# Two groups' gate logits in one set of 512-column products, and two more alignment directives

## The chip, the cores and the metric

The kernel runs on one core of one Trainium2 chip. The metric is the device time of one execution in microseconds; of several runs the median is given. The engines are named as the profile names them: PE (TensorE; PEld its weight loads), DVE (VectorE), ACT (ScalarE), POOL (GpSimd), SP (SyncE, which issues most transfers).

## The reference

```python
# attention: 8 batches x 8 heads, 576 rows in chunks of 64, head size 64
scores = scale * np.matmul(q_c, k_c.transpose(0, 1, 2, 4, 3))
scores = scores - np.max(scores, axis=-1, keepdims=True)
attn = np.exp(scores)
attn = attn / (np.sum(attn, axis=-1, keepdims=True) + 1e-09)
out = np.matmul(attn, v_c)
...
# mixture of experts on its output: x is 4608 x 512, 8 experts, 512 -> 1024 -> 512
logits = x @ w_gate
expert_idx = np.argmax(logits, axis=1)
logits_shift = logits - logits.max(-1, keepdims=True)
probs = np.exp(logits_shift)
probs /= probs.sum(-1, keepdims=True) + 1e-09
gate_w = probs[np.arange(N), expert_idx]
for e in range(E):
    mask = expert_idx == e
    xe = x[mask]
    h = np.maximum(xe @ w1[e], 0.0)
    ye = h @ w2[e]
    out[mask] = gate_w[mask, None] * ye
```

Each row of x goes to the one expert with the largest logit.

## The kernel before, in words

The 4608 rows of x are 36 tiles of 128, taken as 18 groups of G = 2 tiles. The first part is a software pipeline over the groups (the loop at L1033, iteration g = 0 to 17), the second the experts' products, 256 rows and up to 128 more at a time. The order of all engines' work is written out by hand: each engine runs its instructions in the order in which the program issues them.

In iteration g, PE does in this order: scores(g) (L238, 32 products of 64 by 64, into psS); sel_ of group g - 3 (L991: the logits of two tiles, transposed, into psL); attn_t of group g - 1 (L274: eight transposes of the exponentials into psU and psV); x_t of group g - 2 (L310: eight transposes of the rows of x into psT and psQ); in some iterations routing's small products (L379 to L384); attn_v of group g - 1 (L286: attention times v, into psU, psV and, for the last of four head pairs, psT); and logits of group g - 2 (L322). A fp32 product stands in the trace as two matmuls, a transpose as one.

The gate's logits: x_t copies the transposed rows to SBUF (ACT, L312). logits_p multiplies each of the four 128-row pieces of a row's 512 features with its part of the gate's weights, in four column tiles of the array side by side, so that the four partial results lie in four groups of 32 partitions of psL, in columns 128 to 383. ACT copies them to lp (L1007); one iteration later sel_ turns them back into rows, into columns 0 to 127 and 384 to 511 of psL, and sums (DVE, L998) adds the four partial results. Groups make batches of 6, 6, 6, 6, 4, 4, 2 and 2 tiles; when sums has a batch's last group, its routing (route, L327) starts as a generator. Its steps are issued one by one between other work: `small_op` and `advance` take the next step of the first generator that stands at that kind of step, "v" for DVE, "a" for ACT, "t" for PE. A batch's steps fill two iterations. Then its tiles wait for store (L426), in which POOL scatters the rows of x with their gate weight and row number to xd in DRAM, two tiles at the top of each iteration, four in the last, the rest behind the loop. Ahead of that, where tiles wait, POOL copies one column of lp to a scrap tile (relay, L1037), which holds it until lp has been written.

x_out (L298 twice, then L301) divides attn_v's result by the sums that ACT copied (su, L264 and L265) and DVE inverted (ri, L266), and writes the group's rows of x. x_t of the next iteration reads these rows.

When the third batch is routed and its tiles have been stored, the generator early issues the gather of unit 0's rows (L547) into xg; behind the loop make_xt (L570) transposes them and unit 0's products (filler, L622 and L720 to L722) fill the gaps between the last groups' steps. SP issues the loads of q, k and v for coming groups, and in iterations 2 to 10 quarters of an expert's weights.

nc.tensor.addr_align(64, offset=48, max_nops=0) ahead of the scores of g = 3 (and one at L142) sets at which place, counted in instructions modulo 64, the next instruction of PE's code lies; the loader puts padding in between, and with max_nops=0 PE jumps over it with one branch. The second part begins at L1264 with the load of the number of units into registers.

Of the kernel before, what the change touches and what calls it, by code (L numbers as in the profile page):

```python
# [8 lines left out]
F32 = mybir.dt.float32  # L9
# [4 lines left out]
ALU = mybir.AluOpType  # L14
AX = mybir.AxisListType
# [3 lines left out]
P = 128  # L19
# [3 lines left out]
E = 8  # L23
NTILE = NT // P
G = 2
NG = NTILE // G
RB = 4
XB = 5
BATCHES = [6, 6, 6, 6, 4, 4, 2, 2]
NBAT = len(BATCHES)  # L30
NMAX = max(BATCHES)
# [15 lines left out]
def attn_moe_kernel(ctx: ExitStack, tc: tile.TileContext, q, k, v, wg, w, out):  # L47
    nc = tc.nc
# [69 lines left out]
    sp = c1.enter_context(tc.tile_pool(name="sp", bufs=2))  # L118
    sm = c1.enter_context(tc.tile_pool(name="sm", bufs=2))
# [31 lines left out]
    wg_sb = kv.tile([P, 4, 32], F32, name="wg_sb")  # L151
# [3 lines left out]
    first = [sum(BATCHES[:i]) for i in range(NBAT + 1)]  # L155
# [13 lines left out]
    ident = const.tile([P, P], F32, name="ident")  # L169
# [61 lines left out]
    def scores(g):  # L231
        ps = pair
        if g == 3:
            nc.tensor.addr_align(64, offset=48, max_nops=0)
        for i in range(G):
            for hp in range(4):
                for po, m, fo, pi, fi, at_ in quads(i, hp):
                    nc.tensor.matmul(ps[po, m, fo], qt[g][pi, i, fi], kb[g % NK][pi, i, fi],  # L238
                                     start=True, stop=True, tile_position=at_)
        return ps  # L240
# [19 lines left out]
    def soft_d():  # L260
        su = sm.tile([P, NH, 1], F32, name="su", bufs=2)
        ri = sm.tile([P, NH, 1], F32, name="ri", bufs=2)
        for i in range(G):
            nc.scalar.activation(su[:, 6 * i:6 * i + 6, 0], one["UV"[i]][:, i * 64:i * 64 + 326:65], AF.Copy, bias=1e-9)  # L264
            nc.scalar.activation(su[:, 12 + 2 * i:14 + 2 * i, 0], px3[:, i * 195:i * 195 + 66:65], AF.Copy, bias=1e-9)  # L265
        nc.vector.reciprocal(ri.rearrange("p h o -> p (h o)"), su.rearrange("p h o -> p (h o)"))  # L266
        return ri

    def attn_t(ex, banks="UV"):
        at = sp.tile([P, G, 4, 128], F32, name="at", bufs=1)  # L270
# [20 lines left out]
    def x_out(g, ri, xt):  # L291
# [5 lines left out]
        for i in range(G):  # L297
# [4 lines left out]
            o[:, :, 6:8, :], px3[:, 1:261].rearrange("p (i h d) -> p i h d", i=G, d=65)[:, :, :, 0:64],  # L302
            ri[:, 12:NH, :].rearrange("p (i h) o -> p i h o", i=G).broadcast_to([P, G, 2, 64]), ALU.mult)

    def x_t(g, xt):
        xT = sp.tile([P, 4, G * P], F32, name="xT1", bufs=1)
        for i in range(G):
            pxt = bank("TQ", [P, 4, 128])
            for kc in range(4):
                nc.tensor.transpose(pxt[:, kc, :], xt[:, (g * G + i) % RB, kc * 128:(kc + 1) * 128],  # L310
                                    ident)
            nc.scalar.copy(xT[:, :, i * P:(i + 1) * P], pxt)  # L312
        return xT

    pL = bank("L", [P, 512])
    pR = bank("K", [P, 512])

    def logits_p(g, xT):

        pp = pL[:, 128:128 + G * P]  # L320
        for kc in range(4):
            nc.tensor.matmul(pp[kc * 32:(kc + 1) * 32, :], wg_sb[:, kc, :], xT[:, kc, :],  # L322
                             start=True, stop=True, tile_position=(0, kc * 32))
        lp = sp.tile([P, G * P], F32, name="lp", bufs=2)
        return lp, pp

    def route(b, lg):  # L327
# [89 lines left out]
    relay = const.tile([P, 1], F32, name="relay")  # L417
# [14 lines left out]
    active = []  # L432
# [550 lines left out]
    st_e, st_l, st_x = {}, {}, {}  # L983
    casts = []
    lgs = [None]
    p4 = pL.rearrange("p (a t) -> p a t", t=P)

    def sel_(g):
        lp = st_l.pop(g)
        for i in range(G):  # L990
            nc.tensor.transpose(p4[:, 3 * i, :], lp[:, i * P:(i + 1) * P], ident)  # L991

    def sums(g):
        b = [i for i in range(NBAT) if first[i] <= g * G][-1]
        if g * G == first[b]:
            lgs[0] = sm.tile([P, NMAX, E], F32, name="lg", bufs=2)[:, 0:BATCHES[b], :]
        o = g * G - first[b]
        nc.vector.tensor_reduce(lgs[0][:, o:o + G, :],  # L998
                                p4.rearrange("p a (c e) -> p a e c", e=32)[:, 0::3, 0:E, :], AX.X, ALU.add)
        if (g + 1) * G == first[b + 1]:  # L1000
            r = route(b, lgs[0])
            active.append([r, next(r), False])

    def logits(g):
        if g in st_x:
            lp, pp = logits_p(g, st_x.pop(g))
            nc.scalar.copy(lp, pp)  # L1007
            st_l[g] = lp

# [23 lines left out]
    for g in range(NG):  # L1033
        ga, gl = g - 1, g - 2
        pace[0] = 1000
        if waiting:
            nc.gpsimd.tensor_copy(relay, st_l[gl - 1][:, 0:1])  # L1037
        store(2 if g + 1 < NG else 4)
        ps = scores(g)
        keep((6, 0, 0)[min(g, 2)])  # L1040
        if g + NK < NG:
            load_qk(g + NK)
        if g + 1 < NG:
            load_v(g + 1)
        if g == 0:
            nc.sync.dma_start(wg_sb[:, :, 0:E], wg)
        if g == 2:
            nc.gpsimd.memset(oh_b, 0.0)
            for t in (*xg[0], *xg[1], xg3):
                nc.gpsimd.memset(t, 0.0)  # L1050

        if gl >= 1:
            sel_(gl - 1)
        if ga >= 0:
            at = attn_t(st_e[ga])
            if g + 1 == NG:
                st_e[g] = soft_a(ps)
            st_e.pop(ga)
        if gl >= 0:
            st_x[gl] = x_t(gl, xb[gl * G // RB % XB])  # L1060
        if g + 1 < NG:
            st_e[g] = soft_a(ps)
            soft_b(st_e[g])
        else:
            soft_b(st_e[g])

            c2.close()
            psum = ctx.enter_context(tc.tile_pool(name="psum", bufs=1, space=PSUM))
            slots["S"] = [psum.tile([P, 512], F32, name=f"psS{i}") for i in range(2)]
            turns["S"] = 0  # L1070
        if gl >= 1:
            sums(gl - 1)
        pauses()
        for x in casts:
            next(x, None)
        casts.clear()
        advance("t")
        if g + 1 < NG:
            small_op(5)
        if ga >= 0:  # L1080
            attn_v(ga, at)
            ri = soft_d()
        if g + 1 == NG:

            c3.close()
            xtp = ctx.enter_context(tc.tile_pool(name="xtp", bufs=1, side="right", reuse_waits="tile"))
            hp_ = ctx.enter_context(tc.tile_pool(name="hp", bufs=HB, side="right", reuse_waits="tile"))
            xhi = xtp.tile([P, 4, BLK + EXT], F32R, name="xhi")
            xlo = xtp.tile([P, 4, BLK + EXT], F32R, name="xlo")
        logits(gl)  # L1090
        cast(g)
        if ga >= 0:
            x_out(ga, ri, xb[ga * G // RB % XB])
        small_op(2)
        advance("a")
        side_op(4)

    g = NG - 1
# [99 lines left out]
    def slot(u, kp, kr, at_, left):  # L1198
# [62 lines left out]
        finish_x(u, kr, pe)  # L1261
        rest(u, py)

    n_s = nc.values_load(kind[0:1, NU:NU + 1], min_val=0, max_val=SMAX)  # L1264
    on_pe, on_rest = {1: load_kind(1, PE)}, {}
    make_xt_x(1, on_pe[1])
# [46 lines left out]
```

## Time and profile before

| | |
|---|---|
| median of 3 runs (lowest, highest) | 574.78 us (574.77, 575.71) |
| the profiled execution | 572.48 us |
| its span, first to last instruction | 570.2 us |
| mean granted clock of PE | 0.990 of full speed |
| busy share of the span | PE 97%, PEld 86%, DVE 71%, ACT 49%, POOL 42% |
| attention loop | from 5.5 to about 104 us |
| tail, with the last groups and unit 0's first products | to about 131 us |
| DMA, mean over the span | 174 GB/s |

How to read it: busy shares are means over stages with different limits, so the stage that the change touches is read by itself, in the timeline. In the rows below a timeline line has the start, the time from the start of the first to the end of the last instruction of a merged piece, the engine, the line, what it writes and reads, the number of instructions, and in brackets how long the engine was idle ahead of it and what ended that ("issue": nothing that the profile shows). Matmuls overlap, so pieces of PE are compared by their starts.

### The profile page before, as it was taken

What the parts mean: (1) busy time and instruction counts of PE and PEld (TensorE: products, weight loads), DVE (VectorE), ACT (ScalarE), POOL (GpSimd) and SP (SyncE); (2) the same over time, 40 slices, a digit from 0 to 9 for tenths busy, and PEclk for the clock granted to TensorE, in tenths of its full rate; (3) what the DMA queues carried; (4) which work ended last, traced back from release to release, by engine and by line L of the source; (5) the groups of instructions that cost most, each with busy time, mean ns of one, the idle gap of its engine ahead of it and who ended that gap; (6) DMA issues with size and microseconds to landing.
All of it is one profiled execution on the core that took longest, in us unless ns stands there. A gap on an engine that the chain in (4) does not pass through costs nothing.

```text
span 570.2 us, 13170 instructions
## 1 busy us (share of the span) xinstructions
PE 552.2 (97%) x4699; PEld 488.0 (86%) x4699; DVE 405.9 (71%) x907; ACT 281.9 (49%) x519; POOL 239.2 (42%) x271
## 2 busy tenths in 40 slices
PE   7999999869999999999999999999999999999995
PEld 5888888758798899899998999898999988898994
DVE  6788889634776987888867875676757566766663
ACT  5587877522134644646544654354434344444332
POOL 3036753745424553354440843162425235251422
PEclk9999999979999999999999999999999999999998
DMA  8999999333575632236534543465622346211201
GB/s 308 395 366 368 410 408 396 112 123 125 197 252 185 219 99 61 76 115 207 164 94 165 208 123 123 131 236 182 225 58 81 115 152 217 63 42 29 67 1 58
DMA packets 46564, 99.17 MB, mean 174 GB/s; under 512 B 13184, under 2 KB 26496, under 8 KB 42880
## 3 DMA queue, kind: packets, MB, share of 16 engines
q0 software_dynamic: 18352, 58.30, 29.2%
q1 hardware_dynamic: 27824, 38.98, 19.5%
q8 instruction: 67, 1.10, 0.8%
q10 hardware_dynamic: 288, 0.52, 0.2%
q14 instruction: 33, 0.27, 0.1%
HBM read 106.73 MB, written 20.22 MB: 223 GB/s over the span
## 4 chain that ended last, share of the span: by engine, by line
PE 85%; issue 6%; DVE 3%; DMA 2%; POOL 1%; ACT 1%; another core or an unknown queue 0%; POOLq 0%; DVEq 0%; SPq 0%; ACTq 0%
PE psS L622 24%; PE psL L622 8%; PE psU L722 4%; PE psU L720 4%; PE psU L721 4%; PE psV L720 4%; PE psV L721 4%; PE psV L722 4%; PE psS L238 3%; PE psU L286 2%; PE psV L286 2%; PE psL L322 2%; PE psK L735 2%; PE psK L733 2%; PE psS L626 2%
## 5 line engine op out<-in xcount | busy, mean ns | idle before, releaser
L77 DVE TENSOR_TENSOR wlo<-raw,whi 128x1024 fp32r<-128x1024 f32 x110 | 134.3, 1221 | 17.0 <-ACT whi L76 12.2
L671 ACT ACTIVATE h<-psS 128x384 fp32r<-128x384 f32 x84 | 41.3, 492 | 172.5 <-issue 127.6
L529 POOL DMA_INDIRECT raw<-in_w,widx x58 | 66.4, 1145 | 121.3 <-DVE wlo L77 54.1
L622 PE MATMUL psS<-xhi,whi 128*128 128x256 f32 (+2 forms) x368 | 114.4, 313 | 1.4 <-issue 0.7
L76 ACT CAST whi<-raw 128x1024 fp32r<-128x1024 f32 x110 | 114.8, 1043 | 0.3 <-issue 0.3
L622 PE MATMUL psS<-xhi,wlo 128*128 128x256 f32 (+2 forms) x368 | 113.6, 311 | 0.7 <-issue 0.7
L622 PE MATMUL psS<-xlo,whi 128*128 128x256 f32 (+2 forms) x312 | 96.8, 310 | 0.4 <-issue 0.4
L748 POOL DMA_INDIRECT out_y<-y,oid x40 | 42.4, 1060 | 107.0 <-ACTq L653 34.5
L630 DVE SCALAR_TENSOR_TENSOR hl<-psS,h 128x256 fp32r<-128x256 f32 x84 | 35.6, 424 | 59.1 <-ACT h L671 57.2
L547 POOL DMA_INDIRECT xg<-xd,idx x49 | 63.4, 1295 | 30.7 <-issue 16.7
L622 PEld LDWEIGHTS psS<-xhi,whi 128*128 128x128 f32 x368 | 69.9, 190 | 5.4 <-DVE h L630 0.8
L622 PEld LDWEIGHTS psS<-xhi,wlo 128*128 128x128 f32 x368 | 69.7, 189 | 1.5 <-issue 0.9
L622 PEld LDWEIGHTS psS<-xlo,whi 128*128 128x128 f32 x312 | 59.1, 189 | 3.6 <-issue 1.2
L720 PE MATMUL psU<-whi,h 128*128 128x512 f32 x120 | 48.4, 403 | 0.0
L720 PE MATMUL psV<-whi,h 128*128 128x512 f32 x120 | 47.3, 395 | 0.0
L721 PE MATMUL psU<-wlo,h 128*128 128x512 f32 x120 | 47.3, 394 | 0.0
L721 PE MATMUL psV<-wlo,h 128*128 128x512 f32 x120 | 47.1, 393 | 0.0
L722 PE MATMUL psU<-whi,hl 128*128 128x512 f32 x112 | 44.1, 393 | 0.0
L722 PE MATMUL psV<-whi,hl 128*128 128x512 f32 x112 | 44.0, 393 | 0.0
L426 POOL DMA_INDIRECT xd<-xb,di x32 | 31.6, 987 | 16.1 <-issue 12.9
L622 PE MATMUL psL<-xhi,whi 128*128 128x320 f32 (+2 forms) x112 | 34.9, 312 | 0.0
L622 PE MATMUL psL<-xlo,whi 128*128 128x320 f32 (+2 forms) x112 | 34.9, 312 | 0.0
(253 smaller groups left out, 1111.6 us busy)
## 6 DMA issues: line engine op xcount, KB each, us to landing
vb<-in_v SPq DMA_DIRECT2D x36, 260.0 KB
kb<-in_k SPq DMA_DIRECT2D x16, 512.0 KB
qt<-in_q SPq DMA_DIRECT2D x16, 512.0 KB
xg<-xg SPq DMA_DIRECT2D x208, 32.0 KB
raw<-in_w SPq DMA_DIRECT2D x16, 256.0 KB
kb<-in_k SPq DMA_DIRECT2D x4, 256.0 KB
raw<-in_w,widx POOLq DMA_INDIRECT x58
xg<-xd,idx POOLq DMA_INDIRECT x49
```

The source lines that it names most:

```text
L76: nc.scalar.copy(hi, src)
L77: nc.vector.tensor_tensor(lo, src, hi.bitcast(F32), ALU.subtract)
L426: nc.gpsimd.indirect_dma_start(out=xds[t], out_offset=bass.IndirectOffsetOnAxis(ap=di[:, i, :], axis=0), in_=x, in_offset=None, bounds_che ...
L529: nc.gpsimd.indirect_dma_start(out=raw[c][:, :], out_offset=None, in_=w, in_offset=bass.IndirectOffsetOnAxis(ap=widx[:, u, c:c + 1], axis= ...
L547: nc.gpsimd.indirect_dma_start(out=t[:, :], out_offset=None, in_=xd[0:rows, :], in_offset=bass.IndirectOffsetOnAxis(ap=place(u, h), axis=0 ...
L622: nc.tensor.matmul(ph, a, b[:, kc, WIDE - ph.shape[1]:WIDE], start=kc + i == 0, stop=kc + i == 5 and not late)
L630: nc.vector.scalar_tensor_tensor(o, ph, 0.0, hi.bitcast(F32), ALU.max, ALU.subtract)
L671: nc.scalar.activation(hx[:, EXT:EXT + WIDE], ph, AF.Relu)
L720: nc.tensor.matmul(py, hh, wh, start=f == 0, stop=False)
L721: nc.tensor.matmul(py, hh, wl, start=False, stop=False)
L722: nc.tensor.matmul(py, hl, wh, start=False, stop=f == 7)
L748: nc.gpsimd.indirect_dma_start(out=outs[m], out_offset=bass.IndirectOffsetOnAxis(ap=oid[u % 3][:, m:m + 1], axis=0), in_=y, in_offset=None ...
```

## The change

Groups 0 to 15 are taken two at a time. x_t of an even group starts a tile of 512 columns and writes its first half, x_t of the odd group writes the second. logits does nothing for an even group below 16, and for an odd one multiplies all 512 columns, into the whole of psL; the copy to lp is of 512 columns. One iteration later sel_ makes four transposes, and sums adds up both groups, one reduction each, and starts the routing of each batch that ends. Groups 16 and 17 stay by themselves. relay reads the softmax sums where lp has no new entry. A directive with offset 240 modulo 256 stands ahead of the scores of g = 9, one with offset 190 modulo 256 ahead of the second part.

```diff
@@ scores
         if g == 3:
             nc.tensor.addr_align(64, offset=48, max_nops=0)
+        if g == 9:
+            nc.tensor.addr_align(256, offset=240, max_nops=0)
@@ soft_d
+        sus[0] = su
         return ri
@@ x_t, logits_p
+    SOLO = NG - 2
+    xts = [None]
+
     def x_t(g, xt):
-        xT = sp.tile([P, 4, G * P], F32, name="xT1", bufs=1)
+        o = G * P if g % 2 and g < SOLO else 0
+        if not o:
+            xts[0] = sp.tile([P, 4, 2 * G * P], F32, name="xT1", bufs=1)
+        xT = xts[0][:, :, o:o + G * P]
...
-        return xT
+        return xts[0]
...
-        pp = pL[:, 128:128 + G * P]
+        n = (2 if g < SOLO else 1) * G * P
+        pp = pL[:, 0:n]
         for kc in range(4):
-            nc.tensor.matmul(pp[kc * 32:(kc + 1) * 32, :], wg_sb[:, kc, :], xT[:, kc, :],
+            nc.tensor.matmul(pp[kc * 32:(kc + 1) * 32, :], wg_sb[:, kc, :], xT[:, kc, 0:n],
                              start=True, stop=True, tile_position=(0, kc * 32))
-        lp = sp.tile([P, G * P], F32, name="lp", bufs=2)
+        lp = sp.tile([P, 2 * G * P], F32, name="lp", bufs=2)[:, 0:n]
@@ sel_, sums, logits
+    def held(g):
+        return g < SOLO and g % 2 == 0
+
     def sel_(g):
+        if held(g):
+            return
         lp = st_l.pop(g)
-        for i in range(G):
-            nc.tensor.transpose(p4[:, 3 * i, :], lp[:, i * P:(i + 1) * P], ident)
+        if g < SOLO:
+            for i in range(2 * G):
+                nc.tensor.transpose(p4[:, i, :], lp[:, i * P:(i + 1) * P], ident)
+        else:
+            for i in range(G):
+                nc.tensor.transpose(p4[:, G + i, :], lp[:, i * P:(i + 1) * P], ident)
 
     def sums(g):
...
+        if held(g):
+            return
+        for j in (g - 1, g) if g < SOLO else (g,):
...
     def logits(g):
         if g in st_x:
-            lp, pp = logits_p(g, st_x.pop(g))
+            x = st_x.pop(g)
+            if held(g):
+                return
+            lp, pp = logits_p(g, x)
@@ the loop
         if waiting:
-            nc.gpsimd.tensor_copy(relay, st_l[gl - 1][:, 0:1])
+            nc.gpsimd.tensor_copy(relay, st_l[gl - 1][:, 0:1] if gl - 1 in st_l else sus[0][:, 0, :])
@@ ahead of the second part
+    nc.tensor.addr_align(256, offset=190, max_nops=0)
     n_s = nc.values_load(kind[0:1, NU:NU + 1], min_val=0, max_val=SMAX)
```

## Rows read from the trace of the kernel before

**Rows 1.** Busy us by engine in iteration 11; then granted clock, DMA share, GB/s.

```profile
66.40:72.10 5.70, 5.70 (x130) 4.88 (x126) 5.14 (x13) 4.35 (x11) 4.14 (x6) 1.00 1.03 410
```

**Rows 2.** Timeline of PE, from attn_v of iteration 10 to x_t of iteration 11.

```profile
65.47 0.39 PE L286 MATMUL psT<-vb,at 128*64 128x130 f32 x4
65.79 0.64 PE L322 MATMUL psL<-xT,wg_sb 128*32 128x256 f32 x8
66.36 1.16 PE L238 MATMUL psS<-kb,qt 64*64 64x64 f32 x64
67.45 0.44 PE L991 MATMUL psL<-ident,lp 128*128 128x128 f32 x2
67.73 0.60 PE L274 MATMUL psU<-ident,ex 128*128 128x128 f32 x4
...
68.60 0.60 PE L310 MATMUL psT<-ident,xg 128*128 128x128 f32 x4
```

**Rows 3.** Timeline of DVE in the same stretch: the end of x_out.

```profile
67.57 0.41 DVE L301 TENSOR_TENSOR xg<-psT,ri 128x256 f32<-128x256 f32 x1
```

**Rows 4.** Timeline of the tail, DVE and PE: an x_t that waited for x_out.

```profile
124.08 0.41 DVE L301 TENSOR_TENSOR xb<-psT,ri 128x256 f32<-128x256 f32 x1
...
124.55 1.12 PE L310 MATMUL psT<-ident,xb 128*128 128x128 f32 x4 [0.78 <-DVE xb L301]
```

**Rows 5.** Timeline of PE from the last scores to 121 us: pieces behind idle time.

```profile
102.39 0.25 PE L238 MATMUL psS<-kb,qt 64*64 64x64 f32 x1 [0.33 <-issue]
103.12 0.83 PE L238 MATMUL psS<-kb,qt 64*64 64x64 f32 x38 [0.48 <-issue]
...
110.28 0.44 PE L991 MATMUL psL<-ident,lp 128*128 128x128 f32 x2 [0.43 <-ACT lp L1007]
...
116.60 0.64 PE L322 MATMUL psL<-xT,wg_sb 128*32 128x256 f32 x3 [0.34 <-issue]
...
118.06 0.38 PE L622 MATMUL psS<-xlo,whi 128*128 128x256 f32 x1 [0.43 <-issue]
...
119.48 0.38 PE L622 MATMUL psS<-xhi,wlo 128*128 128x256 f32 x1 [0.69 <-issue]
...
120.90 0.28 PE L622 MATMUL psS<-xhi,whi 128*128 128x256 f32 x1 [0.69 <-issue]
```

**Rows 6.** Durations: lines L322, L286 (ns, min/median/max), groups by form (us busy, mean ns).

```profile
L322 PE MATMUL psL<-xT,wg_sb x144: 376/383/404, 19.3 to 129.0; 128*32 128x256 f32 x144
...
L286 PE MATMUL psT<-vb,at x144: 272/273/326, 12.5 to 115.2; 128*64 128x130 f32 x144
...
L312 ACT COPY xT<-psQ 128x512 f32<-128x512 f32 x18 | 10.9, 603 | 0.5 <-PE psQ L310 0.2
...
L1007 ACT COPY lp<-psL 128x256 f32<-128x256 f32 x18 | 6.8, 375 | 5.2 <-issue 2.9 <-PE psL L322 1.8 <-POOL xb L404 0.3
```

**Rows 7.** Timeline of PE: the scores of g = 3, 12 and 13.

```profile
19.83 1.44 PE L238 MATMUL psS<-kb,qt 64*64 64x64 f32 x64
...
72.06 1.31 PE L238 MATMUL psS<-kb,qt 64*64 64x64 f32 x64
...
78.24 1.24 PE L238 MATMUL psS<-kb,qt 64*64 64x64 f32 x64
```

**Rows 8.** Timeline of POOL and PE: batch 2's last scatter, unit 0's gather, its first reader.

```profile
92.45 0.98 POOL L426 DMA_INDIRECT xd<-xg,di  x1 [0.30 <-issue]
100.27 1.04 POOL L547 DMA_INDIRECT xg<-xd,idx  x1 [6.85 <-PE psU L286]
...
110.55 1.12 PE L570 MATMUL psS<-ident,xg 128*128 128x128 f32 x8
```

**Rows 9.** Timeline of PE: its first work behind the first load of the kinds.

```profile
152.53 0.74 PE L605 MATMUL psT<-ident,xg 128*128 128x128 f32 x4 [0.49 <-issue]
```

**Rows 10.** Timeline of PE and DVE, iteration 14: end of attn_v, end of x_out.

```profile
88.82 0.39 PE L286 MATMUL psT<-vb,at 128*64 128x130 f32 x4
...
91.33 0.41 DVE L301 TENSOR_TENSOR xb<-psT,ri 128x256 f32<-128x256 f32 x1
```

More of the change, by code (lines that the diff above doesn't have):

```diff
@@ L266, in soft_d @@
         nc.vector.reciprocal(ri.rearrange("p h o -> p (h o)"), su.rearrange("p h o -> p (h o)"))
+        sus[0] = su
         return ri
+    sus = [None]
     def attn_t(ex, banks="UV"):
@@ L986, in attn_moe_kernel @@
     p4 = pL.rearrange("p (a t) -> p a t", t=P)
+    def held(g):
+        return g < SOLO and g % 2 == 0
     def sel_(g):
+        if held(g):
+            return
         lp = st_l.pop(g)
-        for i in range(G):
-            nc.tensor.transpose(p4[:, 3 * i, :], lp[:, i * P:(i + 1) * P], ident)
-    def sums(g):
[L994 to L1002, printed above, removed]
+        if g < SOLO:
[4 more added lines that the diff above has]
+                nc.tensor.transpose(p4[:, G + i, :], lp[:, i * P:(i + 1) * P], ident)
+    def sums(g):
+        if held(g):
+            return
+        for j in (g - 1, g) if g < SOLO else (g,):
+            b = [i for i in range(NBAT) if first[i] <= j * G][-1]
+            if j * G == first[b]:
+                lgs[0] = sm.tile([P, NMAX, E], F32, name="lg", bufs=2)[:, 0:BATCHES[b], :]
+            o = j * G - first[b]
+            a = G if g >= SOLO else (j % 2) * G
+            nc.vector.tensor_reduce(lgs[0][:, o:o + G, :],
+                                    p4.rearrange("p a (c e) -> p a e c", e=32)[:, a:a + G, 0:E, :], AX.X, ALU.add)
+            if (j + 1) * G == first[b + 1]:
+                r = route(b, lgs[0])
+                active.append([r, next(r), False])
     def logits(g):
         if g in st_x:
-            lp, pp = logits_p(g, st_x.pop(g))
+            x = st_x.pop(g)
+            if held(g):
+                return
+            lp, pp = logits_p(g, x)
             nc.scalar.copy(lp, pp)
```

## The prediction

> **What bounds the kernel now.** I read the page first: its busy line (in the table above) has PE at 97%, so a change must shorten PE's stream, or a place where PE waits. The table by stretches of the attention loop comes next: in one iteration of 5.70 us PE is busy for all of it, DVE for 5.14 us, and the DMA engines show a share of 1.03 [rows 1]. So three things stand close together there: PE is the bound, DVE has about half a microsecond to spare, and the transfers run without a pause. Then the timeline of PE over one turn of the loop, in start times [rows 2]: the last attn_v piece (psT) at 65.47, the logits set of L322 at 65.79, the scores at 66.36, the two transposes of L991 at 67.45, attn_t at 67.73, x_t at 68.60. No idle time stands in it. From the last attn_v piece to x_t are 68.60 - 65.47 = 3.13 us.
>
> The same stretch on DVE is the row that decides: x_out's last operation (L301) runs from 67.57 to 67.98 [rows 3], 2.51 us after that attn_v piece. x_t reads what it writes. Where x_t did wait for it, it began 0.06 us after its end (124.08 + 0.41 = 124.49, then 124.55) [rows 4]. So x_t can begin 2.57 us after the piece at the earliest, and today it is 0.56 us later than that because PE is still busy with logits, scores, L991 and attn_t.
>
> The loop ends near 104 us. Up to 124 us stands a tail in which PE waits, mostly with no releaser that the profile shows ("issue") [rows 5]; after it PE is busy again to the end.
>
> The profiled execution took 572.48 us with a span of 570.2; the runs' median is 574.78, 2.30 more. I work out differences on the profiled rows and add their sum to the median. About 0.2% (1.15 us) is what a measurement of this kernel can tell from no change.
>
> **The change, part by part.** Groups 0 to 15 become eight pairs: iterations with g even (2 to 16) lose the logits set, those with g odd (3 to 17) have one of 512 columns, and the four L991 transposes of a pair stand together in the even iteration after it (the last pair's in the tail).
>
> *Removed.* An iteration without logits loses 66.36 - 65.79 = 0.57 us of PE, and the next one (odd) loses L991's 67.73 - 67.45 = 0.28 [rows 2]. Both lie between attn_v of the even iteration and x_t of the odd one, so PE would reach x_t after 3.13 - 0.85 = 2.28 us. But x_out is ready only after 2.57. I assume that DVE's chain (sums of the softmax on ACT, reciprocal, three products) begins with attn_v's end as before, since nothing in the edit starts it sooner. So the stretch becomes 2.57 us and the saving is 0.56, not 0.85: a wait of 0.29 us for DVE takes the place of the work. Behind the waiting transposes stand routing's matmuls and attn_v, and behind these ACT's copies and the next iteration; all shift with them, so the wait counts in full.
>
> *Added.* The other half of the pair grows. The median matmul of L322 takes 383 ns with 256 columns, that of L286 273 ns with 130 [rows 6]: 0.87 ns a column, 0.22 us for 256 more; a set is two passes over four column tiles side by side, so 0.45 us. No row shows a 512-column matmul of this kind; the bounds are nothing (were the time all fixed cost) and 0.57 (all of the set twice). I take 0.45, since two widths of the same type give it. Two more transposes in a row are 0.22 us, as attn_t's eight take 68.60 - 67.73 = 0.87 us [rows 2]. Together 0.67 us, in a stretch where x_t has PE in front of it for 3.13 us already, so nothing hides it.
>
> Per pair: 0.67 - 0.56 = +0.11 us; eight pairs: +0.88, with bounds of -2.7 and +1.8 from those of the 512-column set. In the last pair x_out has cover: the scores of g = 17 stand still for 0.33 and 0.48 us [rows 5], more than 0.29, so that pair keeps its 0.29: -0.29.
>
> *Moved: the stores.* Batches 0 and 2 end with the even groups 2 and 8, so their routing begins one iteration later, and with it POOL's scatters to xd and the early gather. What gains is the transfers in the middle of the loop: the scores of two iterations were stretched there to 1.31 and 1.24 us [rows 7] from the usual 1.16 [rows 2], and with two scatters fewer ahead of them I give back 0.15 + 0.08: -0.23 (bounds 0 and -0.23). What loses is the gather for unit 0: it was issued from 100.27, after the last scatter it needs (92.45), and PE reads it at 110.55 [rows 8]. One iteration later it would be issued by about 106, so a margin of some 4 us covers it; with that cover gone PE would wait in the tail, by up to 1 us. I count nothing. On POOL the scatters and the gather move past the splits of the weights (L87) and routing's copies, which gain, as they no longer stand behind a gather that waits; SP's queue keeps its order.
>
> *ACT and the tail.* A 512-column copy takes 603 ns [rows 6]; the logits copy took 375 [rows 6], +0.23. In the loop the scores (1.09 us) stand between logits and L991 and hide it. In the tail L991 already waits for that copy (0.43 us, 110.28) [rows 5]: +0.23. The first of the tail's solo sets is unchanged. The relay's new source and the bigger tiles cost nothing: the sums that it reads are written before the logits copy.
>
> *The directives.* Each makes PE jump over padding. The one already there stands ahead of the scores of g = 3, which took 1.44 us [rows 7] instead of 1.16: 0.28. The new one at g = 9 is the same thing in the same place, so +0.28 (bounds 0 and 0.28). The other stands where PE waits 0.49 us for the first kinds anyway [rows 9]; that wait hides it.
>
> [...]
>
> Sum: 0.88 - 0.29 - 0.23 + 0.23 + 0.28 = **+0.87 us**, on the median **575.6 us**, within 0.2%.
>
> **The rivals.**
>
> *A, the forecast,* 575.6; its own range, from the directive, the stores and a few tenths in the 512-column set, is 574.6 to 576.8.
>
> *B, x_out is not late.* Then PE keeps all of 0.85: per pair 0.67 - 0.85 = -0.18, eight times -1.44, with the other terms (-0.23 + 0.23 + 0.28) -1.16: 573.6. For it: x_t has never waited in the steady loop. Against it: 2.51 us from attn_v to the end of L301 is a chain of five dependent steps on two engines, and it stands in every iteration.
>
> *C, the tail's waits without a releaser go away.* Six of them (0.33, 0.48, 0.34, 0.43, 0.69, 0.69) make 2.96 us [rows 5]. All lie in code between the two new directives, so all that code gets another place; and POOL's scatters, which run beside them, shift too. Without them 575.6 - 2.96 = 572.7. For it: no engine, queue or transfer is named as what they wait for, so the code itself is the suspect. Against it: other waits may appear in their stead.
>
> *D, slower: x_out ends later than now.* In the iteration at 88.82 it ended 91.33 + 0.41 [rows 10], 2.92 us after the attn_v piece, so x_t could begin after 2.98 and the saving of a pair is 0.15 instead of 0.56. The place is DVE in the even iterations, which now have two reductions (L998) and often a batch's first steps while PE's work there is shorter. It decides as soon as x_out ends later than 2.5 us after attn_v. In half of the pairs it costs 4 x 0.41 = 1.64: 577.2; in all, 578.9.
>
> *E, nothing of this shows:* what the pairs lose is made up by the transfers; 574.8.
>
> **How the numbers follow.** A 0.40, of which 0.25 within 0.2%, 0.14 slower, 0.01 faster. B 0.08 (0.03 faster, 0.05 the same). C 0.32, faster: six waits without a cause are the largest sum that can move. D 0.16, slower. E 0.04. Together faster 0.36, the same 0.34, slower 0.30. Cases of both signs hold most of the chance, so A's own range is given above; the range for eight in ten reaches from a little under C to D's half: 572.3 to 577.4.
>
> **What would show it.** In the timeline after, the odd iterations' x_t (psT, from ident) should show an idle of about 0.3 us put down to DVE at x_out's last line, eight even iterations without L322, the L322 sets about 1.0 us from start to the scores, and a pair taking some 11.5 us where two iterations take 11.4. Logits of 512 columns should take about 0.6 us each. Wrong would be: no wait at x_t (B); the 102 to 121 us stretch without "issue" (C); x_out ending 3 us after attn_v (D); or the stretch behind the loop longer because PE waits for the gather.

## The result, and the profile after

The changed kernel is slower: 579.03 us against 574.77, medians of 14 runs each (1.0074); the ratio over all runs, which this text gives for every kernel, is 1.0081, with an interval of 1.0058 to 1.0103. The profiled execution took 580.44 us (span 578.4), 7.96 more than the one before, so it shows some losses larger than the medians do. The runs of this study fell on several chips; on some the kernel before takes 574 to 575 us, on others 561, and every ratio is against the kernel before on the same chip.

The busy line of the page:

```profile
PE 552.9 (96%) x4635; PEld 487.6 (84%) x4635; DVE 406.8 (70%) x907; ACT 279.8 (48%) x511; POOL 238.8 (41%) x270
```

PE was busy 0.7 us longer than before, and 8.2 us longer in all: nearly all of the loss is waiting. The waits of PE, in total us, times and longest; those that are new or grew:

```profile
PE psL L1012 <- ACT lp L1035: 3.9, 1, 3.9
PE psU L279 <- DVE xb L303: 1.8, 4, 0.6
...
PE psU L291 <- ACT at L280: 1.3, 3, 0.6
...
PE psU L279 <- ACT whi L85: 0.7, 2, 0.4
```

The second part isn't where it went: from its first product (160.37 below; 152.53 in [rows 9]) to the end it took 418.1 us after and 417.7 before. The last scores, those of g = 17, began at 106.28 and not at 101.44; the tail behind them lost another 3 us (PE waited 9.8 us in it, 6.8 before).

**One undisturbed pair.** The timeline of PE from the end of an odd iteration over an even one (from 38.03) to the start of the next odd one (43.39):

```profile
36.72 0.39 PE L291 MATMUL psT<-vb,at 128*64 128x130 f32 x4
37.04 1.06 PE L334 MATMUL psL<-xT,wg_sb 128*32 128x512 f32 x8
38.03 1.16 PE L240 MATMUL psS<-kb,qt 64*64 64x64 f32 x64
39.13 0.66 PE L1009 MATMUL psL<-ident,lp 128*128 128x128 f32 x4
39.62 0.60 PE L279 MATMUL psU<-ident,ex 128*128 128x128 f32 x4
...
40.50 0.60 PE L321 MATMUL psT<-ident,xb 128*128 128x128 f32 x4
...
43.07 0.39 PE L291 MATMUL psT<-vb,at 128*64 128x130 f32 x4
43.39 1.16 PE L240 MATMUL psS<-kb,qt 64*64 64x64 f32 x64
44.90 0.63 PE L279 MATMUL psU<-ident,ex 128*128 128x128 f32 x4 [0.35 <-ACT whi L85]
...
45.83 0.60 PE L321 MATMUL psT<-ident,xb 128*128 128x128 f32 x4
```

It answers to [rows 2]. The set at the end of the odd iteration and the four transposes behind it: from the psT piece at 36.72 to x_t at 40.50 are 3.78 us, 0.65 more than the 3.13 of before. The set took 38.03 - 37.04 = 0.99 us, 0.42 more. The groups by form give one 512-column product's mean:

```profile
L334 PE MATMUL psL<-xT,wg_sb 128*32 128x512 f32 x64 | 8.5, 605 | 0.0
```

605 ns. The other half: from the psT piece at 43.07 to x_t at 45.83 are 2.76 us, 0.37 less than 3.13. Together +0.28 us a pair. PE's idle time stands ahead of attn_t, not of x_t. What attn_t waited for is seen on DVE, in x_out:

```profile
44.20 0.56 DVE L303 TENSOR_TENSOR xb<-psU,ri 128x384 f32<-128x384 f32 x1
44.67 0.55 DVE L303 TENSOR_TENSOR xb<-psV,ri 128x384 f32<-128x384 f32 x1
45.14 0.41 DVE L306 TENSOR_TENSOR xb<-psT,ri 128x256 f32<-128x256 f32 x1
```

attn_t writes psU and psV, and x_out's first two products read them: psU until 44.20 + 0.56 = 44.76, psV until 45.22. attn_t's first piece began at 44.90, its second at 45.37. The row names ACT's cast, which happened to end in between (the releaser is inferred); in other odd iterations the same wait stands under DVE xb or xg L303, or under "issue".

**Three iterations that are longer still.** The windows of two neighbouring even and odd iterations, and of iterations 13 and 15:

```profile
62.60:67.95 5.35, 5.35 (x120) 4.94 (x116) 3.92 (x7) 4.85 (x11) 3.62 (x5) 1.00 1.01 366
67.95:74.31 6.36, 5.98 (x123) 4.64 (x121) 4.27 (x8) 4.17 (x13) 4.46 (x5) 1.00 1.02 406
79.66:87.40 7.74, 6.76 (x131) 5.02 (x130) 5.25 (x14) 4.38 (x14) 3.88 (x7) 1.00 0.97 363
92.75:100.49 7.74, 6.64 (x131) 5.02 (x129) 7.27 (x16) 3.50 (x12) 3.50 (x5) 1.00 0.96 340
```

The columns are those of [rows 1]. The first two are undisturbed: 5.35 us for an even and 6.36 for an odd iteration are what the pair above gives. The odd iterations 7 (with routing's products) took 6.66; but 9, 13 and 15, which have them too, took 7.21, 7.74 and 7.75: 0.55, 1.08 and 1.09 more, 2.7 us together. In iteration 15 DVE's busy time is 7.27 us. Where that comes from, on POOL and then on DVE:

```profile
93.69 1.00 POOL L438 DMA_INDIRECT xd<-xb,di  x1 [0.55 <-issue]
95.00 0.98 POOL L438 DMA_INDIRECT xd<-xb,di  x1 [0.30 <-issue]
96.00 1.28 POOL L87 TENSOR_TENSOR wlo<-raw,whi 128x512 fp32r<-128x512 f32 x1
```

```profile
95.36 1.96 DVE L505 TENSOR_TENSOR ge<-ge,st 128x6 f32<-128x6 f32 x1
...
97.62 1.22 DVE L255 TENSOR_REDUCE mx<-psS 128x16 f32<-128x1024 f32 x1
```

L505, a product of 6 columns in early's chain, is put down as 1.96 us and ends at 97.32, with POOL's split of a weight (L87, until 97.28). Its counterpart before:

```profile
85.72 0.17 DVE L493 TENSOR_TENSOR ge<-ge,st 128x6 f32<-128x6 f32 x1
```

0.17 us. The softmax's maximum (mx, at 97.62) stands behind it on DVE, and the next scores, attn_t and ACT's exponentials behind that. In this profile the delay shows in iteration 16, which took 5.78 us and not 5.35. What lengthened iteration 15 itself is the thing that is seen in iteration 13. PE, then ACT, DVE and POOL:

```profile
79.66 1.16 PE L240 MATMUL psS<-kb,qt 64*64 64x64 f32 x64
81.16 0.63 PE L279 MATMUL psU<-ident,ex 128*128 128x128 f32 x4 [0.34 <-DVE xb L303]
...
84.17 0.89 PE L291 MATMUL psU<-vb,at 128*64 128x130 f32 x12 [0.41 <-ACT at L280]
```

```profile
81.96 0.21 ACT L384 ACTIVATE eg<-psK 128x48 f32<-128x48 f32 x1 [1.38 <-DVE xb L306]
83.53 0.59 ACT L280 COPY at<-psU 128x512 f32<-128x512 f32 x1 [1.36 <-PE psQ L321]
```

```profile
83.42 1.23 DVE L255 TENSOR_REDUCE mx<-psS 128x16 f32<-128x1024 f32 x1 [1.25 <-PE psQ L321]
```

```profile
80.52 1.01 POOL L438 DMA_INDIRECT xd<-xb,di  x1 [0.55 <-issue]
81.83 0.97 POOL L438 DMA_INDIRECT xd<-xb,di  x1 [0.30 <-issue]
```

attn_t's first four transposes end at 81.79; the copy on ACT that waits for them starts at 83.53. The maximum on DVE needs scores that ended at 80.82; it starts at 83.42. Both engines stood idle, and both went on at the same time. Both wait for PE's semaphore, and the trace has no update of it between 79.75 and 83.39, and then five within 0.3 us. (The trace has 479 updates of it for 534 instructions that make one, so the gap alone would say little; the two idle engines are the evidence.) By this reading PE's signals arrived up to 2.6 us late, while POOL issued two scatters. attn_v (84.17) then had to wait for the copy. In iteration 15 the same stands on PE and ACT:

```profile
97.26 0.89 PE L291 MATMUL psU<-vb,at 128*64 128x130 f32 x12 [0.64 <-ACT at L280]
```

```profile
96.62 0.59 ACT L280 COPY at<-psU 128x512 f32<-128x512 f32 x1 [1.36 <-PE psK L396]
```

The transposes that this copy waits for ended at 94.88.

**The tail.** POOL, then a copy on ACT, and the readers on PE:

```profile
104.09 0.98 POOL L438 DMA_INDIRECT xd<-xg,di  x1 [0.30 <-issue]
...
108.18 1.06 POOL L559 DMA_INDIRECT xg<-xd,idx  x1 [2.90 <-PE psS L240]
...
113.93 1.06 POOL L438 DMA_INDIRECT xd<-xg,di  x1 [1.92 <-DVE ri L268]
```

```profile
128.24 0.17 ACT L267 ACTIVATE su<-psT 128x2 f32<-128x2 f32 x1 [5.50 <-remote]
```

```profile
114.43 1.13 PE L582 MATMUL psS<-ident,xg 128*128 128x128 f32 x8
...
128.87 0.69 PE L1012 MATMUL psL<-ident,lp 128*128 128x128 f32 x2 [3.94 <-ACT lp L1035]
...
160.37 1.04 PE L617 MATMUL psT<-ident,xg 128*128 128x128 f32 x4 [0.77 <-issue]
```

The gather for unit 0 was issued at 108.18, 7.9 us later than in [rows 8], and PE read it at 114.43 without a wait. But the scatters behind it began at 113.93 instead of 106.75. The wait for lp behind it, 1.67 us at 123.08 in the profile before, is now 3.94 us: the copies on ACT ahead of lp begin at 128.24, though the attn_v pieces that they read had ended by 119.86, and 1.4 us after the end of POOL's row of scatters (126.83). Before, the copy began at 122.46, the pieces had ended by 115.49 and the row at 121.09: again 1.4 us. So the wait moved with the end of the row. Within it the granted clock of PE fell from 1.00 to 0.50 for 6.8 us, from 126.5 (before: from 121.5); PE's wait had begun at 124.93 (before: at 121.41).

### The profile page after: what moved, and what is told of

Its sections match the earlier page's. It is cut to its first block, busy times and chain, and to the rows that moved or that the text cites. A ratio compares the mean times of both kernels' runs of the same rounds, so it can differ in the third digit from the quotient of the medians.

```text
span 578.4 us, 13016 instructions
## 1 busy us (share of the span) xinstructions
PE 552.9 (96%) x4635; PEld 487.6 (84%) x4635; DVE 406.8 (70%) x907; ACT 279.8 (48%) x511; POOL 238.8 (41%) x270
## 4 chain that ended last, share of the span: by engine, by line
PE 79%; DVE 8%; issue 5%; ACT 3%; another core or an unknown queue 2%; POOL 1%; POOLq 0%; DVEq 0%; ACTq 0%
PE psS L634 23%; PE psL L634 8%; PE psU L734 4%; PE psV L732 4%; PE psV L733 4%; PE psV L734 4%; PE psU L732 4%; PE psU L733 4%; PE psS L240 2%; PE psK L747 2%; PE psK L745 2%; PE psL L334 2%; PE psV L291 1%; PE psU L291 1%
```

## The experiments

**E1: without the two new directives.**

```diff
-        if g == 9:
-            nc.tensor.addr_align(256, offset=240, max_nops=0)
...
-    nc.tensor.addr_align(256, offset=190, max_nops=0)
```

> The changed kernel without its two new alignment directives. Theory (late rows): the loss of some 4.5 us is 8 pairs at about 0.28 us each (PE stands 0.35 us ahead of attn_t in the odd iterations, because the buffer psU is still read by x_out) and for the rest the scatters of batches 0 and 2, which come one iteration later, with unit 0's gather behind them; the place of the code matters little: 579 us, within 1 us of the changed kernel, and the iterations from 55, 80 and 93 us stay long (7.2 to 7.8 us). Rival (code placement): the directives put PE's code where it stalls; without them 576 us or less, and these three iterations fall to 6.7 us.

566.28 us against 561.17, ratio 1.0069 [1.0048, 1.0091]. The iteration from 55 us is 6.66, but from 73 us on five in a row are long (6.71, 7.17, 5.99, 7.32, 6.13). The directives aren't the loss. Two of these five, 15 and 16 (7.32 and 6.13), follow from a long product of early, 1.87 us here; see E13.

**E2: late routing alone, in the kernel before.**

```diff
+        todo, late[:] = late[:], []
         if (g + 1) * G == first[b + 1]:
-            r = route(b, lgs[0])
+            (late if b in (0, 2) else todo).append((b, lgs[0]))
+        for b, lg in todo:
+            r = route(b, lg)
             active.append([r, next(r), False])
```

> The kernel before, with the routing of batches 0 and 2 begun one iteration later and nothing else: no pairs, no new directives. Theory (late rows): unit 0's gather is issued about 6 us later (106 rather than 100 us), the last burst of scatters behind the loop ends later by as much, and PE waits for it: 576.5 to 577.5 us. Rival (pairs alone): the late rows cost nothing, 574.8 us within 0.6.

561.96 against 561.17, 1.0009 [0.9997, 1.0021]. The gather did move, to 105.0 us, and PE then waited for later gathers at the start of the second part (the waits of PE):

```profile
PE psQ L570 <- DMA xg<-xd,idx: 1.2, 1, 1.2
...
PE psT L605 <- DMA xg<-xd,idx: 0.8, 1, 0.8
```

2.0 us of waits, but hardly any time lost: late rows by themselves are worth 0.1%, at most 0.2%, on a chip of this kind. That part of my theory fell here; it was not run on a chip of the other kind, where the tail's wait moves with the scatters.

**E3: three tiles at a time.**

```diff
-        store(2 if g + 1 < NG else 4)
+        store(3 if g in (14, 15) else 2 if g + 1 < NG else 4)
```

> The changed kernel, with three tiles stored instead of two at the top of iterations 14 and 15, so that batch 2 is stored one iteration sooner. Theory (late rows): the gather comes at about 101 us again, the burst behind the loop ends some 4 us sooner, and 2 to 3 us of the loss come back: 576 to 577 us. Rival (pairs alone, or code placement): 579 us as the changed kernel.

562.43 against 561.17, 1.0026 [1.0009, 1.0042], well under E1 on the same chip. All iterations are 5.35, 6.35 or 6.65 us, and L505 took 0.17: three scatters in a row had moved L87 away from it.

**E4 and E9: plain transfers in place of the loop's scatters.**

```diff
+            if plain:
+                nc.sync.dma_start(xds[t][t * P:(t + 1) * P, :], x)
+                continue
```

> The changed kernel with the scatters of iterations 8 to 16 replaced by plain transfers of the same rows from SP's queue, to places in their own order, so the experts then work on other rows than the routing chose; scatters behind the loop stay. Theory (late rows): the stalls in the odd iterations with routing come while POOL issues scatters, so the iterations from 55, 80 and 93 us fall from 7.2 to 7.8 us to 6.7, and 574 to 577 us in all. Rival (code placement): the three iterations stay at 7.2 to 7.8 us.

> The changed kernel with the scatters of iterations 8 to 16 as plain transfers from SP's queue, once more (the experts then work on other rows than the routing chose). Theory (held signals): in the profile of the changed kernel the completion signals of PE reach ACT and DVE up to 2.6 us late while POOL issues scatters, and this makes the iterations from 55, 80 and 93 us 0.55, 1.1 and 1.1 us longer; without scatters in the loop they are 6.65 us each and the last scores start about 2.7 us sooner (103.5 instead of 106.2). Rival (pairs alone): no change in these three. A chip on which the signals are not held shows neither.

E4: 564.14 against 561.17, 1.0048 [1.0029, 1.0066]; E9: 564.49 against 561.14, 1.0053 [1.0038, 1.0068]. Both fell on chips of the 561 us kind, in none of whose twelve profiles a copy or maximum of the loop waits as in iteration 13 above. So the question of the signals stays open. The product of early took 0.17 us, but iteration 15 was still 7.43 and 7.44. The cause stands in iteration 14, on DVE and on POOL (E4):

```profile
87.15 1.18 DVE L497 TENSOR_TENSOR_SCAN c<-ce 128x3 f32<-128x3 f32 x1
```

```profile
87.05 1.27 POOL L87 TENSOR_TENSOR wlo<-raw,whi 128x512 fp32r<-128x512 f32 x1 [0.16 <-ACT whi L85]
```

Another small operation of early, a scan that took 0.20 us in the kernel before, lasts until L87 ends (88.33, 88.32), with no scatter near; x_out is then late, and attn_t of iteration 15 waits 1.13 us for it. E9 has the same (1.19 us). Its iteration 9 (7.60) is another thing: the scores stood still for 1.14 us, with no releaser.

**E5 and E13: the changed kernel again.** No edit.

> The changed kernel as it is, as a control on the chip of the experiments. If the pairs cost what their rows show (8 x 0.28 = 2.2 us) and the rest are stalls that vary from chip to chip, it stands here nearer to the kernel before than 0.8%: some 0.3 to 0.5%. If the late rows of batch 2 are the cause of half the loss, it stands at 0.7 to 0.8%, clearly above the run with three tiles at a time (0.26%).

> The changed kernel as it is, beside the next three. On a chip whose profile shows the signals of PE held while POOL issues scatters: 0.6 to 0.8% over the kernel before, with long iterations from 55, 80 and 93 us. On one that does not: the fixed cost of eight pairs at 0.28 us, 2.2 us or 0.40%, and iterations of 5.35, 6.35 and 6.65 us. A value of 0.7% or more there would leave 1.5 us unexplained.

E5: 577.71 against 574.00, 1.0062 [1.0041, 1.0083], with the same three long iterations (7.02, 7.82, 7.83). E13, on a chip of the other kind: 564.47 against 561.09, 1.0058 [1.0042, 1.0074]. There 9 and 13 have their undisturbed 6.65, but iteration 14 took 6.66 (its scores stood still for 1.00 us, with no releaser), 15 took 7.31, 16 took 6.13 and L505 1.86. What L505 cost is seen here without late signals. PE in iteration 16:

```profile
99.21 1.16 PE L240 MATMUL psS<-kb,qt 64*64 64x64 f32 x64 [0.60 <-DVE ex L256]
101.03 0.66 PE L1009 MATMUL psL<-ident,lp 128*128 128x128 f32 x4 [0.66 <-ACT lp L1035]
```

Iterations 15 and 16 are 0.67 and 0.78 us over 6.64 and 5.35, together 1.45 us; E1 and E14 have the same two lengths within 0.01 us.

**E6: the two directives alone, in the kernel before.**

```diff
+        if g == 9:
+            nc.tensor.addr_align(256, offset=240, max_nops=0)
...
+    nc.tensor.addr_align(256, offset=190, max_nops=0)
```

> The kernel before with the two new directives and nothing else. Theory (pairs and late rows): no change within 0.15%; the jump at g = 9 may cost up to 0.28 us. Rival (code placement): the directives by themselves move the time by 1 us or more, either way.

576.11 against 574.00, 1.0041 [1.0022, 1.0059]: the rival held here. The scores of g = 9 show no jump (1.16 us). What is longer is iteration 12, with 7.55 us instead of 6.18. PE, then ACT:

```profile
77.18 0.89 PE L288 MATMUL psU<-vb,at 128*64 128x130 f32 x12 [0.99 <-ACT at L277]
```

```profile
73.94 0.21 ACT L374 ACTIVATE eg<-psK 128x48 f32<-128x48 f32 x1 [0.66 <-DVE xb L300]
76.54 0.58 ACT L277 COPY at<-psU 128x512 f32<-128x512 f32 x1 [2.39 <-PE psK L386]
```

attn_v waits for ACT's copy, and ACT stood idle 2.39 us ahead of it: once more an iteration with routing's products and scatters, and the form of iteration 13 above. Whether the directives bring this stall about isn't shown: E17, without them, has such iterations too.

**E7 and E8: the changed kernel without one or the other directive.** The edits are the two halves of E1's.

> The changed kernel without the directive ahead of the second part; the one at g = 9 stays. Theory: as the changed kernel within 0.15%. Rival (code placement of the second part): the time from the second part's first instruction to the end, 418.1 us in the changed kernel's profile and 416.4 to 417.1 in the four runs so far, moves by 0.5 us or more.

> The changed kernel without the directive at g = 9; the one ahead of the second part stays. If placing the code of the loop matters, this run has the long iterations (over 7 us from 80 us on) of the run without both directives and stands some 0.4% above the control; if not, it is equal to the control.

E7: 577.09, 1.0062 [1.0042, 1.0083]; E8: 578.49, 1.0073 [1.0057, 1.0089], both against 574.00 and beside E5's 1.0062. Neither can be told from E5, with intervals of some 0.2% either way. The second part took 416.4 us in E5 and 417.8 in E8 with the second directive, 416.8 in E7 and 417.1 in E1 without. Within the changed kernel the directives explain none of the loss.

**E10 and E11: the odd iterations' scatters later.** The relay reads the reciprocals (E10) or x_out's last product (E11).

```diff
-        sus[0] = su
+        sus[0] = ri
```

> The changed kernel, in which the odd iterations' relay reads the reciprocals instead of the sums, so that their scatters start about 0.6 us later, as far behind the scores as in the kernel before (1.5 instead of 0.9 us). Theory (held signals, decided by when the scatter starts): the three long iterations shrink by half or more, 1.5 to 2.5 us back. Rival: it is the pairs' lack of slack, wherever the scatter stands: no change within 0.2%.

> The same with the relay reading x_out's last product: the odd iterations' scatters start some 2.9 us behind the scores. Theory (when the scatter starts): the long iterations are gone, or the wait moves to x_out, where a hold of 1 to 2 us behind attn_v would show as a late reciprocal. Rival (slack): no change within 0.2%.

E10: 563.46 against 561.14, 1.0043 [1.0029, 1.0058], all iterations undisturbed (5.35, 6.33 to 6.71). DVE's product of E10:

```profile
93.11 0.17 DVE L505 TENSOR_TENSOR ge<-ge,st 128x6 f32<-128x6 f32 x1
```

0.17 us, while L87 ran from 94.39. E11: 564.47, 1.0049 [1.0036, 1.0063]; L505 is short there too, but another small operation of routing (L403, which adds 1e-9) took 2.01, 1.62 and 0.91 us at 60.8, 85.1 and 98.3 us, each time until L87 ended. The collision moves with what stands beside L87. The theory itself, of late signals, was not put to the test on this chip, and no run of the changed kernel stands beside these two; E13's 1.0058, on another chip, is within their intervals.

**E12: earlier scatters in the kernel before.** The relay reads the sums in every iteration.

> The kernel before with every relay reading the softmax sums, so that its scatters start some 0.7 us sooner, as in the odd iterations of the changed kernel. Theory (when the scatter starts): 1 to 3 us slower on a chip on which the signals are held. Rival (slack): the loop of the kernel before has half a microsecond to spare in every iteration, no change within 0.2%.

561.35 against 561.14, 1.0014 [0.9995, 1.0033]. The rival (slack) stands: early scatters alone cost the kernel before nothing that shows. The run fell on a chip without late signals, so for the other kind nothing follows.

**E14: the transposes of four pairs two and two.**

```diff
         if held(g):
+            if g - 1 in HALF:
+                for i in (2, 3):
+                    nc.tensor.transpose(p4[:, i, :], kept[0][:, i * P:(i + 1) * P], ident)
             return
...
-            for i in range(2 * G):
+            for i in range(G if g in HALF else 2 * G):
```

> The changed kernel, in which four pairs, those whose odd group ends no batch, have their L1009 transposes two and two: the even group's in the even iteration, the odd group's in the odd one, ahead of attn_t. Theory (PE stands 0.35 us ahead of attn_t in odd iterations because psU is still read by x_out): the two moved ones cost nothing there, each of these four pairs takes 0.22 us less, 0.88 us or 0.15% under the changed kernel beside it; the wait shows as 0.14 us. Rival (PE has no such room): no change, the odd iterations grow by 0.22 us.

563.68 against 561.09, 1.0051 [1.0034, 1.0069], 0.07% under E13 beside it, which is no difference that can be told. The rows can. PE in an odd iteration that got two transposes (L1009), scores first:

```profile
42.53 1.16 PE L240 MATMUL psS<-kb,qt 64*64 64x64 f32 x64
43.63 0.44 PE L1009 MATMUL psL<-ident,lp 128*128 128x128 f32 x2
44.05 0.63 PE L279 MATMUL psU<-ident,ex 128*128 128x128 f32 x4
```

From scores to attn_t are 44.05 - 42.53 = 1.52 us with the two transposes; without them it was 44.90 - 43.39 = 1.51. They stood in room that was there. The even iteration that lost them took 5.13 instead of 5.35, 0.22 us less, as said.

**E15 and E17: the kernel before with three tiles at a time,** in iterations 13 and 14, so that batch 2 is stored sooner and the gather issued at 97.5 us.

> The kernel before with three tiles stored instead of two in iterations 13 and 14, so that unit 0's gather is issued in iteration 14, about 94 us. Theory (in the run of the changed kernel with the same edit, an earlier gather gave some 0.2% back): 0.5 to 1.5 us faster than the kernel before. Rival: the tail is bound by the last groups' chain and not by POOL: no change within 0.2%.

> The kernel before with three tiles stored in iterations 13 and 14, once more, beside the pairs with the same edit. 0.26% faster than the kernel before as in its first run, 0.15 to 0.4%; the iterations of the loop 5.7 and 6.03 us, the last scores about 76.5 us behind those of g = 4.

E15: 560.16 against 561.09, 0.9974 [0.9961, 0.9988], faster than both kernels. E17 on a chip of the other kind: 573.84 against 575.16, 0.9991 [0.9963, 1.0019], not told from no change. Its profile has long iterations too (7.80 and 7.73).

**E16 and E18: pairs with the edits together.** E16 has those of E3, E10 and E14, E18 those of E3 and E10.

> The changed kernel with three edits that are tried apart: three tiles at a time in iterations 14 and 15, the relay of odd iterations from the reciprocals, the transposes of four pairs two and two. Theory: 2.2 us of pairs less 0.9 for the transposes and about 1 for the earlier gather, so 0 to 0.2% over the kernel before. Rival (the pairs cost more than their rows): 0.3% or more.

> The changed kernel with three tiles stored in iterations 14 and 15 and the odd iterations' relay from the reciprocals. Both edits keep early's product (L505) out of the way of POOL's split of a weight (L87), so that it takes 0.17 us and not 1.9; iterations 5.35, 6.35 and 6.65 us throughout. Theory (the pairs by themselves cost 0.28 us each): 2.0 to 2.3 us, 0.35 to 0.4%, above the run beside it, so 0.1 to 0.2% above the kernel before. Rival (the pairs cost what the changed kernel loses): 0.6% or more above the run beside it.

E16: 563.25 against 561.09, 1.0049 [1.0030, 1.0068]: the terms did not add up. L505 is short in its profile, and of the loop only iterations 11 and 14 are longer (by 0.4 and 0.7 us), yet the median is where E14's is. E18: 576.89 against 575.16, 1.0035 [1.0010, 1.0060]. L505 took 0.17 us, as said, but the iterations did not keep to their lengths: 11 took 7.85 and 15 took 8.10 us. E18 lies 0.44% by the ratios, 3.05 us by the medians (0.53%), above E17 beside it. That is between the theory's 0.4% and the rival's 0.6%, with an interval that holds both. Nor is the pairing all that differs: E17 stores its three tiles one iteration sooner, and its gather is issued at 98.58, E18's at 105.21. In the two profiles the tail (last scores to the second part) is 7.0 us longer in E18 and the loop 0.8 us shorter.

## Why the prediction was wrong, by its own steps

575.6 us was forecast, with a range up to 577.4; 579.03 came. The sum had +0.87 us, and the medians show +4.26. Two steps failed: the wait in the half of a pair that loses work, and the moved stores, which I put at nothing.

*The removed half of a pair* is the first. I let x_t begin 2.57 us after the psT piece, since x_t reads x_out's last product, and priced the wait at 0.29. But attn_t stands ahead of x_t, and it writes psU and psV, which x_out's first two products still read. So PE stops one step earlier, and x_t came after 2.76 us: 0.37 saved, not 0.56. E14 shows the room in which PE waits. *The added half* was right: 0.42 for the set (0.45 said), 0.22 for the transposes, 605 ns a product (about 0.6 said). A pair costs 0.28 us and not 0.11, eight of them 2.2 us and not 0.88: 1.4 us of the error. E10, in which the rest of the loop is undisturbed, lies 2.3 us over the kernel before.

*The last pair's cover* (-0.29) wasn't there: attn_t of g = 17 waited 0.55 us like the others.

*The stores* had two terms. The scores of g = 12 and 13 fell back to 1.16 us, as said. What I costed at nothing went wrong, the relay's new source first. An odd iteration has no fresh lp, its relay reads the sums, and its scatters start 80.52 - 79.66 = 0.86 us after the scores, where they stood 1.5 us after them before. So L87 comes to lie on early's product. In all seven profiles of the changed order with the stores and the relay as they were, that product took 1.86 to 1.96 us; in all thirteen others 0.17:

| kernel | L505, us | scores of g = 4 to g = 17, us | ratio |
|---|---|---|---|
| before | 0.17 | 75.63 | 1 |
| changed | 1.96 | 79.92 | 1.0081 |
| E5, E13: changed | 1.95, 1.86 | 79.82, 79.49 | 1.0062, 1.0058 |
| E1, E7, E8: fewer directives | 1.87, 1.95, 1.95 | 80.72, 79.81, 81.13 | 1.0069, 1.0062, 1.0073 |
| E14: transposes two and two | 1.87 | 78.48 | 1.0051 |
| E3: three tiles | 0.17 | 76.75 | 1.0026 |
| E10, E11: relay later | 0.17, 0.17 | 76.89, 78.33 | 1.0043, 1.0049 |
| E4, E9: plain transfers | 0.17, 0.17 | 77.89, 79.08 | 1.0048, 1.0053 |
| E16, E18: edits together | 0.17, 0.17 | 77.20, 79.84 | 1.0049, 1.0035 |

Pairs with the long product lie at 1.0051 to 1.0081, those with the short one at 1.0026 to 1.0053. The lengths of the loop are from one profile each, and on the slower kind of chip they vary: E17, an unpaired loop, has 80.63. A clean pair loop is 76.75 (E3); the seven with the collision are 1.7 to 4.4 us longer, not all of it by the one product. On the chips of the 561 us kind the parts can be added: 2.2 us for the pairs and 1.45 for L505 where it is long, less 0.9 for E14's transposes. That makes 3.7 for E13, 2.2 for E10 and 2.8 for E14, and the medians are 3.4, 2.3 and 2.6 us over the kernel before. E16 doesn't fit: with E15's gain of 0.9 us for the earlier gather it should be at 0.4, and its median is at 2.2. On the chip of the result L505 accounts for about 0.4 us (iteration 16), since iteration 15 was held by late signals already.

*The gather*, too, stood at nothing. Unit 0's gather itself was covered, as said. But the row of scatters behind it ended 5.7 us later, and the wait for lp grew from 1.67 to 3.94 us. No profile of the 561 us kind has this wait.

*ACT and the tail*: L1009 in the tail waits for nothing, since attn_t now stands ahead of it (113.06, then 113.99): neither +0.23 nor the old 0.43. *The jump at g = 9*: 1.16 us, no price in the changed kernel; E6 shows 0.41% with the two directives in the other kernel, so "0 to 0.28" was no bound. Nor was 0.28 the price of the old jump: the scores of g = 3 stand behind it in every run, and took 1.16 us in E2, E4, E6 and E12.

Of the rivals, *D* named the right sign and place (what stands between attn_v and x_t in the odd iterations), but its mechanism, a late x_out, isn't what the rows show: x_out ended 45.55 - 43.07 = 2.48 us after the piece, as before. (In iteration 15 of E4 and E9 x_out was late indeed, held up by L87.) *C* got 0.32: of its six waits (2.96 us) three are left in that stretch (1.87 us), but the wait for lp, which has a releaser, took more than they gave.

Open is the part of the signals, to which, by the profiles, most of what is left of the 4.26 us belongs. On the chip of the result, in E5, E7 and E8, iterations 13 and 15 lost 1.1 to 1.2 us each at the same places, with PE's signals late while POOL issues scatters. E9 to E12, made to test it, fell on chips that don't show it. E18 is the one run with later scatters on the slower kind: its iterations 9 and 13 took 6.66 and 6.71 us, where those four profiles have 7.00 to 7.21 and 7.74 to 7.84, but another, 11, was held. E18 also stores three tiles at once, so that the start of the scatters decides it is possible and not shown.

## What to carry to other kernels

When work is taken off the engine that bounds, ask not only when the next reader's data is ready but when every buffer that the next writers overwrite comes free: the step that was safely late is now early. Joining two steps into one double step saves only its fixed part, here 0.15 us of 1.14 a pair; it has to pay for the iteration left short. A throttle that is tied to some result (the relay here) is part of the schedule: a new source moves all that it holds back.

## What the runs showed of the hardware

Some small operations of DVE lasted until POOL's tensor product L87 ended, to within 0.06 us: L505 (6 columns) took 1.86 to 1.96 us instead of 0.17 in seven profiles (in the changed kernel's it ended at 97.32, L87 at 97.28), L403 0.91 to 2.01 us in E11, L497 (a scan of 3 columns) 1.18 and 1.19 us in E4 and E9. L505 began up to 0.64 us ahead of L87 (95.36 against 96.00), and still ended with it. It began in the second of two scatters (95.00), right ahead of L87. In the kernel before it began in the first of two (85.72, the scatter at 85.43) and took 0.17, so a scatter by itself doesn't hold it. What holds these operations, and why the wait begins ahead of L87, no run here shows.

On one kind of chip the kernel before took 574 to 575 us, on the other 561. On the first, ACT and DVE went on up to 2.6 us after the end of the work of PE that they waited for, in the loop and while POOL issued scatters (iteration 13: 80.82, then 83.42), which is read above as late signals of PE. Seven of its eight profiles show this (not the one of the kernel before), and in the loop none of the twelve of the other kind. The second part took 416.3 to 419.3 us on both kinds. The difference lies in the tail: 48.0 to 55.0 us from the last scores to the second part on the slower kind, 38.1 to 42.2 on the other. On the slower kind PE waited 1.67 to 5.63 us in the tail for lp, on the other not at all. In seven of the eight profiles of the slower kind the granted clock fell to 0.50 in the tail, where PE had been waiting; on the other kind it stayed at 1.00 to within some 6 us of the program's end.
